# One product of the down projection over both token halves from seven inner products, with sums made by accumulating DMAs

## The chip, the cores and the metric

The kernel runs on one core of one Trainium2 chip. The metric is the device time of one execution in microseconds. The engines are named as the profile names them: PE is TensorE (matmuls), DVE is VectorE, ACT is ScalarE, POOL is GpSimd, and SP only issues DMAs.

## The reference

A token's output mixes a linear attention block `a` and a gated linear unit `b` by a scalar gate `g`. Token count is 2048, width 640, inner width 1536, 32 heads of 20.

```python
x = A_x
g = sigmoid((x * gate_w).sum(-1, keepdims=True))
# a: phi(t) = where(t > 0, t + 1, exp(t)) + 1e-6 of q and k; kv = sum over tokens of phi(k) v
#    o = phi(q) kv / (phi(q) sum phi(k) + 1e-6); a = o @ wo
# b: h = sigmoid(x @ w_gate) * (x @ w_up); b = h @ w_down
return g * a + (1 - g) * b
```

All of it is float32.

## The kernel before

Every float32 product is made from three matmuls: each operand is split in a high part (ACT rounds it, line 215) and a low part (DVE subtracts, line 219), and PE adds high x high, high x low and low x high in PSUM (`mm3`, lines 203 and 205). A matmul has a 128x128 weight and 512 moving columns.

Up to about 510 us the kernel computes the attention's sums, then the gated unit in 12 blocks of 128 rows of `h`, already weighted by `1 - g`; blocks of `phi(q)`, weighted by the attention's factor, are put beside them as further rows, so that one **down projection** gives the sum of both branches. Its weights are `w_down` and the attention's matrix `m`.

The down projection is done in two token halves (`pr` 0 and 1), each of two groups of 512 tokens. Even and odd row blocks and the two token groups make a 2x2 scheme of Strassen's kind, with seven products instead of eight. Their operands on the side of `h` are called B11, B21, T2, T1, T3, B22 and T4: the T forms are sums and differences of h blocks, made on DVE in the gated part and stored to DRAM by POOL (`h_dram`, for each form and half 8 blocks of 128 rows by 512 tokens). On the weight side `sum_s` has stored the sums that belong to them (`s_dram`).

From 510.8 us on only this projection runs. It goes by **h tiles**: an h tile is two of the 8 blocks of one form (128 x 2 x 512 values, 512 KB). Tiles are numbered in the order in which PE takes them; `HQ` is that list, 56 tiles long before the change. For each tile SP loads it into one of three raw buffers (`hw`, `load_h`); ACT and DVE split it into one of five split buffers (`hf`, `queue_h`, `NH = 5`), so that tile k takes the buffer of tile k-5; after the split SP issues the load of tile k+3 into the raw buffer that came free. PE then takes it with the weights of two or three output blocks of 128 columns: 12 or 18 matmuls. Weights come the same way, through two raw buffers `ws` into `wa`. A fifth output block is kept in PSUM tiles `rot`; the others are in `cc`, `dd` and `ch`, two buffers each. When the last tile of a product is done, ACT copies a PSUM tile out (`ot<-ch` and the like) or DVE adds it to an earlier result; POOL stores the finished output (`put`).

T3 is multiplied with the second and fourth output block's weights (`USE["T3"] = ("SE", (1, 3), None)`): for each half 4 tiles of 12 matmuls.

What stands where in an engine's list is decided when the program is written out, by `Order`: it keeps a running estimate of the time of PE, ACT and DVE, and `fill` puts a waiting split into the lists of ACT and DVE when the estimate says that its load has landed (8 us after it was issued, for most tiles) and that it ends no more than a few us behind PE. What PE needs for its next matmul and has not yet been put in is put in at that point (`need`). Engines run their lists in order.

```python
SEQ = [[(1, "B11"), (0, "B11")], [(1, "B21")], [(1, "T4")], [(0, "B21")]]
SEQ += [[(pr, n)] for pr in (1, 0) for n in ("T2", "T1", "T3", "B22")] + [[(0, "T4")]]
HQ = [(pr, n, pp) for turn in SEQ for pp in range(PP) for pr, n in turn]
```

Of the kernel before, what the change touches and what calls it, by code (L numbers as in the profile page):

```python
# [7 lines left out]
F32 = mybir.dt.float32  # L8
# [7 lines left out]
P = 128  # L16
# [162 lines left out]
def gated_mix_kernel(ctx: ExitStack, tc: tile.TileContext, xt, xn, wk, wv, wo, wst_q, wst_f, out_t):  # L179
# [81 lines left out]
    s_dram = [dram.tile([P, 2, TG], F32, name=f"s{p}") for p in range(FC // 2 + 2)]  # L261
    r_dram = [dram.tile([P, 2, TG], F32, name=f"r{pr}") for pr in range(2)]
# [1115 lines left out]

    def raw_down(odd, pp):
# [159 lines left out]
    hooks = {0: begin, 3: den_all}  # L1539
    NH = 5  # L1540
    WA, RAW = {}, {}

    def wd_tile(key, cols):
        pool = PL["ha"] if key == ("E", 0) else PL["wa"]
# [4 lines left out]
    def load_down(key, t=None):  # L1549
# [3 lines left out]
        if kind == "S":  # L1553
            v = t[:, :8 * P].rearrange("p (j o c) -> p j o c", j=2, c=P)
            nc.sync.dma_start(t[:, :8 * P].rearrange("p (j c) -> p j c", j=2), s_dram[n])
# [8 lines left out]
        RAW[key] = v, max(order.pe, order.vec) + (8.0 if kind == "S" else 5.0)  # L1564

    d_loads = [("E", pp) for pp in range(1, PP)] + [("O", pp) for pp in range(4)] + [("L", 0)]
    d_loads += [("S", p) for p in range(2 * PP)]
# [5 lines left out]
    def queue_down(key):  # L1573
# [5 lines left out]
        def s_part(j):  # L1579
            t = wd_tile((("SE", "SO")[j], n // 2), 4)  # L1580
            split(t[:, 0, n % 2], t[:, 1, n % 2], RAW[key][0][:, j])
            if j:
                order.then(next_down)
# [5 lines left out]
        def whole():  # L1589
            if kind == "L":  # L1590
                t = WA[key] = PL["wa"].tile([P, 2, KC + 2, P], F32R, name="wl", tag="wl")
            else:
                t = wd_tile(key, 3 if kind == "E" else KC)
            split(t[:, 0], t[:, 1], RAW[key][0])
            if key != ("E", 0):
                order.then(next_down)

        if kind == "S":
            for j in range(2):
                order.add(a_cost(4 * P), v_cost(4 * P), lambda j=j: s_part(j), ("wa", ("SE", "SO")[j], n // 2), at)  # L1600
        else:
            w = {"E": 6, "O": 10, "L": 7}[kind] * P
# [4 lines left out]
    SEQ = [[(1, "B11"), (0, "B11")], [(1, "B21")], [(1, "T4")], [(0, "B21")]]  # L1607
    SEQ += [[(pr, n)] for pr in (1, 0) for n in ("T2", "T1", "T3", "B22")] + [[(0, "T4")]]
    HQ = [(pr, n, pp) for turn in SEQ for pp in range(PP) for pr, n in turn]
    HF, HR = {}, {}  # L1610

    def load_h(k, tiles=None):
        if k < len(HQ):
            pr, n, pp = HQ[k]
            if tiles:
                for i, t in enumerate(tiles):
                    nc.sync.dma_start(t, h_dram[pr, n][:, 2 * pp + i])
            else:
                tiles = PL["hb"].tile([P, 2, TG], F32, name="hw", tag="hw", bufs=3)
                nc.sync.dma_start(tiles, h_dram[pr, n][:, 2 * pp:2 * pp + 2])  # L1620
            HR[k] = tiles, max(order.pe, order.vec) + (5.0 if k < 5 else 8.0)

# [15 lines left out]
    REST, REST_AT = {}, {13: 0, 20: 1, 36: 0}  # L1638
# [110 lines left out]
    plan += [("S", p) for p in range(2 * PP)]  # L1749
# [4 lines left out]
    hk = done_h = 0  # L1754

    def advance():

        while plan:
# [7 lines left out]
            else:  # L1766
                order.stream = order.mid if kind == "S" else order.items
# [7 lines left out]
    USE = {"B11": ("E", (0, 1), 2), "B21": ("O", (0, 2), 4), "T2": ("SE", (0, 2), None), "T1": ("SO", (1, 3), None),  # L1775
           "T3": ("SE", (1, 3), None), "B22": ("SO", (0, 2), None), "T4": ("O", (1, 3), None)}
# [5 lines left out]
    def mm(ps, wt, wp, col, h, first):  # L1782
# [4 lines left out]
    class Pass:  # L1787
# [23 lines left out]
        def product(self, q, pp, h):  # L1811
            if q is not None:
                mm(self.dst[q], WA[self.kind, pp], (0, 1), self.cols[q], h, self.first and pp == 0)
            elif self.extra is not None:
                mm(self.extra, WA[self.ek, pp], (0, 1), self.ec, h, self.n in ("B11", "B21") and pp == 0)
# [25 lines left out]
        def out(self, q):  # L1841
            pr, n, C = self.pr, self.n, self.C
            if q is not None:
                ps = self.dst[q]
                if n in ("B11", "T2", "T1") or self.own:
                    C[n, q] = out_tile()
                    act(C[n, q], ps, AF.Copy, "q")
                elif n == "T4":
                    self.close(q, ps)
                else:  # L1850
                    o, g = {"B21": (0, self.g0), "T3": (1, self.g1), "B22": (0, self.g1)}[n]
                    t = C.pop(({"B21": "B11", "T3": "T1", "B22": "T2"}[n], q))
# [99 lines left out]
```

## Time and profile before

| | |
|---|---|
| Median of 3 runs | 726.13 us (726.11 to 726.49) |
| Profiled execution | 727.02 us, of which the span is 724.2 |
| First matmul of the down projection | 510.76 us into the span |
| Last matmul | 719.99 us, then the last output block leaves |
| Granted PE clock | 1.00 all through |
| DMA | 144.05 MB, mean 199 GB/s |

The page of the profile gives each engine's busy share of the span. A group's row names the source line, the engine, the operation and what it writes and reads, then the count, the busy time, the mean of one in ns, and what ended the idle time ahead of it. In a timeline row the first two numbers are the start and the duration in us; in brackets stands how long the engine had been idle, and on whom it had waited. A row of the DMA view ends with the median time from issue to landing. In a table of stages each engine's busy time stands with its count of instructions, and the last three columns are the granted clock, the DMA share and GB/s.

### The profile page before, as it was taken

To read this page: it belongs to the slowest core of one execution; us is meant where nothing else is said; L and a number is where in the kernel's file an instruction comes from. 1 tells how busy PE (TensorE), PEld (TensorE's weight loads), DVE (VectorE), ACT (ScalarE), POOL (GpSimd) and SP (SyncE) were. 2 spreads that over 40 slices of the span, in tenths; PEclk is the share of its full clock that TensorE was granted. 3 is DMA by queue.
4 is the path that set the end of the run, shared out by engine and by line. 5 is a ranking of instruction groups with operands and counts; after the bars stand their busy time and mean duration, and the time that the engine had idled before them with its cause. 6 is when DMAs were issued, how large, how long until landed. Compare 5 with 4: busy or idle time off the path is not lost.

```text
span 724.2 us, 9524 instructions
## 1 busy us (share of the span) xinstructions
PE 719.5 (99%) x3411; PEld 607.8 (84%) x3411; DVE 486.3 (67%) x773; ACT 320.5 (44%) x541; POOL 128.9 (18%) x221
## 2 busy tenths in 40 slices
PE   9999999999999999999999999999999999999997
PEld 8999998888888888888888888888888888888886
DVE  4878576868764698678879778786866664434340
ACT  6664637166756233333333232334367644424321
POOL 0311011122520023213224222330200000010000
PEclk9999999999999999999999999999999999999999
DMA  7553536897555474556578658474987975565431
GB/s 253 140 141 70 162 55 159 201 302 247 191 174 182 153 238 126 176 194 242 188 273 299 221 188 294 157 258 143 324 300 259 329 231 190 158 213 194 146 113 72
DMA packets 59491, 144.05 MB, mean 199 GB/s; under 512 B 7310, under 2 KB 20782, under 8 KB 59445
## 3 DMA queue, kind: packets, MB, share of 16 engines
q1 hardware_dynamic: 40757, 88.50, 38.4%
q0 software_dynamic: 18544, 54.83, 23.2%
q8 instruction: 26, 0.43, 0.3%
q14 instruction: 20, 0.16, 0.1%
q10 hardware_dynamic: 144, 0.13, 0.1%
HBM read 89.81 MB, written 49.84 MB: 193 GB/s over the span
## 4 chain that ended last, share of the span: by engine, by line
PE 99%; DVE 0%; ACT 0%; issue 0%
PE ch L205 18%; PE cc L205 17%; PE rot L205 16%; PE dd L205 14%; PE ch L203 9%; PE cc L203 8%; PE rot L203 8%; PE dd L203 7%; PE cc L1136 1%; PE rot L300 0%; PE cc L1216 0%; DVE ot L219 0%; ACT ot L215 0%
## 5 line engine op out<-in xcount | busy, mean ns | idle before, releaser
L219 DVE TENSOR_TENSOR hf<-hw,hf 128x1024 fp32r<-128x1024 f32 x54 | 65.8, 1223 | 68.7 <-ACT hf L215 68.4
L215 ACT ACTIVATE hf<-hw 128x1024 fp32r<-128x1024 f32 x54 | 56.8, 1057 | 53.7 <-PE rot L205 30.5
L219 DVE TENSOR_TENSOR c<-cc,c 128x512 f32<-128x512 f32 x56 | 37.7, 686 | 45.9 <-PE cc L205 40.5
L205 PE MATMUL dd<-hf,wa 128*128 128x512 f32 x160 | 49.3, 389 | 0.0
L205 PE MATMUL ch<-hf,wa 128*128 128x512 f32 x160 | 49.3, 389 | 0.0
L1736 POOL DMA_DIRECT2D out_t<-ot x18 | 9.7, 540 | 183.8 <-DVE ot L219 180.8
L215 ACT ACTIVATE wG<-wst 128x640 fp32r<-128x640 f32 x17 | 12.4, 737 | 65.0 <-PE dd L205 65.0
L215 ACT ACTIVATE c<-ch 128x512 f32<-128x512 f32 x32 | 19.1, 597 | 48.8 <-PE ch L205 44.0
L205 PE MATMUL rot<-hf,wa 128*128 128x512 f32 x128 | 39.4, 389 | 0.0
L205 PE MATMUL cc<-hf,wa 128*128 128x512 f32 x128 | 39.4, 389 | 0.0
L203 PE MATMUL dd<-xrh,wG 128*128 128x512 f32 x90 | 35.3, 393 | 0.0
L205 PEld LDWEIGHTS ch<-hf,wa 128*128 128x128 f32 x160 | 30.0, 188 | 6.3
L205 PEld LDWEIGHTS dd<-hf,wa 128*128 128x128 f32 x160 | 30.0, 188 | 6.3
L205 PE MATMUL dd<-xrh,wG 128*128 128x512 f32 x90 | 35.1, 390 | 0.0
L205 PE MATMUL dd<-xrl,wG 128*128 128x512 f32 x90 | 35.0, 389 | 0.0
L219 DVE TENSOR_TENSOR c<-c,om 128x512 f32<-128x512 f32 x48 | 33.1, 692 | 1.6
L203 PE MATMUL cc<-xbh,wS 128*128 128x512 f32 x84 | 32.7, 389 | 0.0
L205 PE MATMUL cc<-xbl,wS 128*128 128x512 f32 x84 | 32.7, 389 | 0.0
L205 PE MATMUL cc<-xbh,wS 128*128 128x512 f32 x84 | 32.7, 389 | 0.0
L203 PE MATMUL dd<-hf,wa 128*128 128x512 f32 x80 | 31.1, 389 | 0.0
L203 PE MATMUL ch<-hf,wa 128*128 128x512 f32 x80 | 31.1, 389 | 0.0
L215 ACT ACTIVATE c<-rot 128x512 f32<-128x512 f32 x24 | 14.2, 597 | 38.1 <-PE rot L205 30.8
(471 smaller groups left out, 2084.6 us busy)
## 6 DMA issues: line engine op xcount, KB each, us to landing
hf<-p_dram SPq DMA_DIRECT2D x16, 512.0 KB, 4.7
hw<-h1T SPq DMA_DIRECT2D x16, 512.0 KB, 5.4
hw<-h0T SPq DMA_DIRECT2D x16, 512.0 KB, 4.3
wst<-wst_f SPq DMA_DIRECT2D x12, 640.0 KB, 4.7
xst<-xt SPq DMA_DIRECT2D x10, 640.0 KB, 7.0
h1T<-c POOLq DMA_DIRECT2D x24, 256.0 KB, 2.7
h0T<-c POOLq DMA_DIRECT2D x24, 256.0 KB, 3.0
hw<-h1B SPq DMA_DIRECT2D x11, 512.0 KB, 4.5
```

The source lines that it names most:

```text
L203: nc.tensor.matmul(o, l_hi, r, start=first, stop=False, skip_group_check=True)
L205: nc.tensor.matmul(out, a, b, start=False, stop=last and n == 1, skip_group_check=True)
L215: nc.scalar.activation(out, src, fn, **kw)
L219: nc.vector.tensor_tensor(out, a, b, op=op)
L1136: nc.tensor.matmul(ps[:w, b0:b1], v[:, m, :w], g(m), start=(m == 0), stop=(m == KC - 1))
L1736: (eng or nc.gpsimd).dma_start(out_t[o * P:(o + 1) * P, g * TG + c0:g * TG + c1], t[:, c0:c1])
```

## The change

T3's two products, one for each token half, are seen as one product of a 2x2 scheme again: the two output blocks by the two halves of the 8 row blocks, times those two halves of the rows by the two token halves. It is formed in Strassen's way from seven **inner products** P1 to P7 of four row blocks each, that is of two h tiles each, and an inner tile feeds 6 matmuls.

- The operands of P7, P6 and P3 are sums of T3 of both halves. They are made in DRAM (`f_sum`, in two parts) by POOL's DMAs that add to what is there: `f_copy` and `f_add` before P7, another `f_add` between P7 and P6, another between P6 and P3. P5's operand is made in place in `h_dram[0, "T3"]` by `f_low`.
- The weights of the inner products (kind `I`, two sets) are loaded from `s_dram` in four DMAs each; DVE makes four sums of them, and they are split like others. `S` loads now leave out those columns (two DMAs for one). E's weights are split in two parts, `E` and `E2`.
- The results are combined on DVE: P7's, P1's, P6's and P5's are copied out by ACT and added into the PSUM tiles `dd` and `cc` in which P2, P3 and P4 also add up (`Inner.out`, `x_sums`). T3's eviction in `Pass.out` goes; T1's second pass now closes the output blocks that T3 closed.
- The order of tiles is new. After tile 19 (the end of B21 for half 0) come, with + for half 1: P7 P7 T2+ P1 T2+ P1 T2+ T2+ P6 T2 P6 T2 P5 T2 P5 T2 P2 P2 P3 T1+ P3 T1+ P4 T1+ P4 T1+, tiles 20 to 45; then B22+, T1, B22 and T4 as whole products, to tile 61.

```diff
+    f_sum = dram.tile([P, 4, TG], F32, name="f_sum")
...
+    KA, KB = (slice(0, 2), slice(2, 7, 4)), (slice(3, 5), slice(5, 8, 2))
+    KF = (slice(0, 2), slice(2, 4))
...
+    def f_copy(u):
+        nc.gpsimd.dma_start(f_sum[:, KF[u]], h_dram[1, "T3"][:, KA[u]])
+
+    def f_add(u, pr, c):
+        nc.gpsimd.dma_start(f_sum[:, KF[u]], h_dram[pr, "T3"][:, c[u]], accum_op=OP.add)
+
+    def f_low(u):
+        h = h_dram[0, "T3"]
+        nc.gpsimd.dma_start(h[:, KA[u]], h[:, KB[u]], accum_op=OP.add)
...
-    hooks = {0: begin, 3: den_all}
+    hooks = {0: begin, 3: den_all, 5: lambda: f_copy(0), 6: lambda: f_add(0, 0, KA), 11: lambda: f_low(0)}
...
+        elif kind == "I":
+            def at_i():
+                return at() if done_h > 8 else 1e9
+            order.add(a_cost(2 * P), v_cost(2 * P), lambda: i_plain(0), ("wa", "I", n), at_i)
+            order.add(a_cost(4 * P), v_cost(4 * P), lambda: i_plain(1), ("wa", "I", n), at_i)
+            for s in range(4):
+                order.add(0, v_cost(2 * P), lambda s=s: i_sum(s), ("wa", "I", n), at_i)
+            for s in (2, 3):
+                order.add(a_cost(4 * P), v_cost(4 * P), lambda s=s: i_plain(s), ("wa", "I", n), at_i)
...
-    HQ = [(pr, n, pp) for turn in SEQ for pp in range(PP) for pr, n in turn]
+    HQ = [(pr, "B11", pp) for pp in range(PP) for pr in (1, 0)]
+    HQ += whole(1, "B21") + whole(1, "T4") + whole(0, "B21")
+    HQ += mixed("P7 P7 T2+ P1 T2+ P1 T2+ T2+ P6 T2 P6 T2 P5 T2 P5 T2 P2 P2 P3 T1+ P3 T1+ P4 T1+ P4 T1+")
+    HQ += whole(1, "B22") + whole(0, "T1") + whole(0, "B22") + whole(0, "T4")
+    INNER = {"P7": (f_sum, KF), "P6": (f_sum, KF), "P3": (f_sum, KF), "P1": (h_dram[1, "T3"], KA),
+             "P2": (h_dram[1, "T3"], KB), "P5": (h_dram[0, "T3"], KA), "P4": (h_dram[0, "T3"], KB)}
...
+            nxt = {"P7": ("P6", 0, KB), "P6": ("P3", 1, KB)}.get(n)
+            if nxt:
+                key = nxt[0], pp
+                F_DUE[key] = lambda: f_add(pp, *nxt[1:])
+                order.late.append((HR[k][1], lambda: F_DUE.pop(key, int)()))
...
-    REST, REST_AT = {}, {13: 0, 20: 1, 36: 0}
+    REST, REST_AT = {}, {13: 0, 28: 1, 50: 0}
+    F_AT = {6: lambda: f_copy(1), 9: lambda: f_add(1, 0, KA), 20: lambda: f_low(1)}
...
+        def product(self, u, h):
+            w = WI[self.n, u]
+            prod(self.dst, [(w[:, 0, i], w[:, 1, i], h[:, 0, i], h[:, 1, i]) for i in (0, 1)], self.first and u == 0)
+
+        def out(self):
...
+            elif n in ("P2", "P3"):
+                q = int(n == "P3")
+                t = CS[1].pop(("T4", q))
+                add(t, X[1][q], t, "q")
+                put(2 * q + 1, 2, t)
+            if n in IS:
+                act(IS[n], self.dst, AF.Copy, "q")
+            if n == "P6":
+                add(IS["P1"], IS["P6"], IS["P1"], "a")
+                sub(IS["P7"], IS["P1"], IS["P7"])
+                add(X[1][1], X[1][1], IS["P7"])
+            elif n == "P5":
+                add(X[1][1], X[1][1], IS["P5"], "a")
+                add(IS["P5"], IS["P5"], IS["P1"])
...
+    def x_sums(pr):
+        if pr:
+            add(X[1][0], X[1][0], IS["P1"])
+        else:
+            sub(X[0][0], X[0][0], IS["P1"])
+            sub(X[0][1], X[0][1], IS["P5"])
```

How this moves instructions is shown at three places. The numbers in the names are those of buffers in the built program: in the changed kernel the split tiles 20 to 25 are hf_5216, hf_5238, hf_5282, hf_5322, hf_5353 and hf_5372.

ACT, from the eviction of the second column of B21 (half 0) on. Before the change, this was the end of B21 and the start of T2:

```order
L215 ACTIVATE ot_5282<-ch_5166 128x512
L215 ACTIVATE hf_5302<-hw_5232 128x1024
L215 ACTIVATE rot_5307<-ot_4871 128x512
L215 ACTIVATE hf_5321<-hw_5243 128x1024
L215 ACTIVATE hf_5344<-hw_5271 128x1024
```

After the change, at the same place; wa_5379 is the weight of P5's and P7's second tiles, wa_5293 and wa_5359 are those of P1, P2 and P3, and is_5391 takes P7's result:

```order
L215 ACTIVATE ot_5336<-ch_5208 128x512
L215 ACTIVATE hf_5353<-hw_5241 128x1024
L215 ACTIVATE wa_5293<-ws_5271 128x256
L215 ACTIVATE wa_5359<-ws_5271 128x512
L215 ACTIVATE hf_5372<-hw_5285 128x1024
L215 ACTIVATE wa_5379<-ws_5271 128x512
L215 ACTIVATE wa_5381<-ws_5271 128x512
L215 ACTIVATE is_5391<-ch_5365 128x512
```

Four weight splits of the second set of inner weights now stand there, two of them behind the split of tile 25 (hf_5372), which takes the buffer of tile 20.

DVE at the same place. Before, with the closing sums of B21 and the low parts of tiles 23 to 25 (hf_5268, hf_5302 and hf_5321):

```order
L219 TENSOR_TENSOR hf_5268<-hw_5188,hf_5268 128x1024
L219 TENSOR_TENSOR ot_4898<-ot_5282,ot_4898 128x512
L219 TENSOR_TENSOR ot_5295<-rot_5167,ot_4911 128x512
L219 TENSOR_TENSOR hf_5302<-hw_5232,hf_5302 128x1024
L219 TENSOR_TENSOR hf_5321<-hw_5243,hf_5321 128x1024
```

After, from B21's last closing sum (ot_5349, which reads `rot`) on; ws_5271 are the raw inner weights, on which the sums are made in place:

```order
L219 TENSOR_TENSOR ot_5349<-rot_5209,ot_4930 128x512
L219 TENSOR_TENSOR hf_5353<-hw_5241,hf_5353 128x1024
L219 TENSOR_TENSOR wa_5293<-ws_5271,wa_5293 128x256
L219 TENSOR_TENSOR wa_5359<-ws_5271,wa_5359 128x512
L219 TENSOR_TENSOR ws_5271<-ws_5271 128x256 x2
L219 TENSOR_TENSOR hf_5372<-hw_5285,hf_5372 128x1024
L223 SCALAR_TENSOR_TENSOR ws_5271<-ws_5271 128x256
L219 TENSOR_TENSOR ws_5271<-ws_5271 128x256
L219 TENSOR_TENSOR wa_5379<-ws_5271,wa_5379 128x512
```

Three low parts of weights and four sums have come in between, and wa_5379 stands last.

DVE where a product closes. Before, T3 of half 1 (sums from dd_4660 and dd_4661) among the low parts of B22's tiles:

```order
L219 TENSOR_TENSOR ot_5466<-dd_4660,ot_5466 128x512
L219 TENSOR_TENSOR ot_5139<-dd_4660,ot_5139 128x512
L219 TENSOR_TENSOR hf_5546<-hw_5488,hf_5546 128x1024
L219 TENSOR_TENSOR ot_5477<-dd_4661,ot_5477 128x512
L219 TENSOR_TENSOR ot_5155<-dd_4661,ot_5155 128x512
```

After, from P5's end (its result is ot_5585) to P3's; the tiles 35 to 40 are hf_5589 (T2's last), hf_5602 and hf_5623 (P2), hf_5636 (P3), hf_5649 (T1+) and hf_5672 (P3); P2 closes in dd_4667 and P3 in dd_4668:

```order
L219 TENSOR_TENSOR dd_4668<-dd_4668,ot_5585 128x512
L219 TENSOR_TENSOR ot_5585<-ot_5585,is_5391 128x512
L219 TENSOR_TENSOR hf_5589<-hw_5532,hf_5589 128x1024
L219 TENSOR_TENSOR hf_5602<-hw_5555,hf_5602 128x1024
L219 TENSOR_TENSOR cc_4688<-cc_4688,is_5391 128x512
L219 TENSOR_TENSOR cc_4689<-cc_4689,ot_5585 128x512
L219 TENSOR_TENSOR hf_5623<-hw_5577,hf_5623 128x1024
L219 TENSOR_TENSOR ot_5169<-dd_4667,ot_5169 128x512
L219 TENSOR_TENSOR hf_5636<-hw_5592,hf_5636 128x1024
L219 TENSOR_TENSOR hf_5649<-hw_5605,hf_5649 128x1024
L219 TENSOR_TENSOR hf_5672<-hw_5626,hf_5672 128x1024
L219 TENSOR_TENSOR ot_5187<-dd_4668,ot_5187 128x512
```

Sums that read a product which PE has just closed now stand directly ahead of the low part of the tile that PE takes next; behind the last row comes hf_5685, tile 41. On ACT the high part of hf_5589 stands behind P5's eviction, that of hf_5602 behind the eviction of T2's first column, and that of tile 46 (B22's first) behind T1's second.

More of the change, by code (lines that the diff above doesn't have):

```diff
@@ L1563, in load_down @@
                 nc.sync.dma_start(v[:, j], src[:, j])
-        RAW[key] = v, max(order.pe, order.vec) + (8.0 if kind == "S" else 5.0)
+        RAW[key] = v, max(order.pe, order.vec) + (8.0 if kind in "SI" else 5.0)
     d_loads = [("E", pp) for pp in range(1, PP)] + [("O", pp) for pp in range(4)] + [("L", 0)]
-    d_loads += [("S", p) for p in range(2 * PP)]
+    d_loads += [("S", p) for p in range(2 * PP)] + [("I", u) for u in range(2)]
     def next_down():
@@ L1766, in advance @@
             else:
[L1767 removed]
+                order.stream = order.mid if kind in "SI" else order.items
                 queue_down((kind, k))
```

187 lines of the change are left out of this document (140 added, 47 removed).

## The prediction

> **What bounds the kernel now.** I read the page first: the share of the engines and the chain of work that ended last. Then the waits of TensorE, then the timeline around the place where the first changed product will stand, about 592 us.
>
> ```profile
> span 724.2 us, 9524 instructions
> PE 719.5 (99%) x3411; PEld 607.8 (84%) x3411; DVE 486.3 (67%) x773; ACT 320.5 (44%) x541; POOL 128.9 (18%) x221
> ...
> PE 99%; DVE 0%; ACT 0%; issue 0%
> ...
> PE rot L300 <- PEq L1943: 0.8, 1, 0.8
> ```
>
> The last row is the whole answer on what PE waited for: 0.8 us, once, at the start. So before the change the end is set by the matmuls alone, and everything else lies beside them. A removed matmul is worth its full pace; an added wait on PE costs its full length.
>
> ```profile
> 592.36 0.39 PE L203 MATMUL dd<-hf,wa 128*128 128x512 f32 x1
> 592.59 0.62 PE L205 MATMUL dd<-hf,wa 128*128 128x512 f32 x2
> 593.04 0.39 PE L203 MATMUL dd<-hf,wa 128*128 128x512 f32 x1
> ```
>
> The duration of 0.39 us is pipelined; the pace is what counts. Three matmuls start between 592.36 and 593.04, so one costs 0.227 us. 592.36 us is also the start of tile 20, which was T2's first and becomes P7's first.
>
> **What is removed.** T3 was 8 tiles (4 for each token half) of 12 matmuls, 96. Now 14 tiles (7 inner products of two tiles) of 6 matmuls, 84. 12 fewer, 12 x 0.227 = **2.7 us saved**. All else on PE keeps its count.
>
> **What is added beside PE.** Six more tiles to load and split, and the splits are the point:
>
> ```profile
> L219 DVE TENSOR_TENSOR hf<-hw,hf 128x1024 fp32r<-128x1024 f32 x54 | 65.8, 1223 | 68.7 <-ACT hf L215 68.4
> L215 ACT ACTIVATE hf<-hw 128x1024 fp32r<-128x1024 f32 x54 | 56.8, 1057 | 53.7 <-PE rot L205 30.5
> L219 DVE TENSOR_TENSOR c<-cc,c 128x512 f32<-128x512 f32 x56 | 37.7, 686 | 45.9 <-PE cc L205 40.5
> L219 DVE TENSOR_TENSOR ws<-ws 128x256 f32<-128x256 f32 x1 | 0.4, 417 | 0.0
> hw<-h1T SPq DMA_DIRECT2D x16, 512.0 KB, 5.4
> ```
>
> A split is 1.06 us on ACT, then 1.22 us on DVE; a sum of 512 columns is 0.69 us, of 256 columns 0.42 us; a load lands 5.4 us after its issue. An h tile had fed 12 matmuls or more (2.7 us of PE); an inner tile feeds 6 (1.36 us), and with T2's tiles between them the mean is 2.04 us. With three raw buffers a tile can come every (5.4 + 1.06 + 1.22) / 3 = 2.6 us. Five split tiles of lead cover some of that; the lead is used up about where P5 stands. As totals ACT and DVE have room (44% and 67%); what counts is where a split stands in their order, since each engine runs its list in order.
>
> How eviction and PE touch is seen before the change:
>
> ```profile
> 588.48 0.60 ACT L215 ACTIVATE ot<-ch 128x512 f32<-128x512 f32 x1 [3.60 <-PE ch L205]
> ...
> 591.88 1.06 ACT L215 ACTIVATE hf<-hw 128x1024 fp32r<-128x1024 f32 x1 [0.76 <-PE rot L205]
> ...
> 592.56 0.69 DVE L219 TENSOR_TENSOR ot<-rot,ot 128x512 f32<-128x512 f32 x1 [0.68 <-PE rot L205]
> ```
>
> Each starts when PE is done with its bank or tile: the last, 592.56, lies 0.2 us after the next tile's first matmul at 592.36. An eviction is 0.60 us on ACT. In this part of the before kernel the split that runs is for a tile four or five ahead, so an eviction in front of it cost PE nothing. With the new order this cover is gone at seven or eight places; I lay the rows of the new order out in time with the durations above, a row starting when the row ahead of it and what it reads are done (the engine's pace is some 0.1 us shorter than a duration).
>
> *Gap 1, the second tile of P7.* Its weight (wa_5379) is split last of the weights, from sums. On ACT that split stands behind the split of hf_5372, and hf_5372 takes the buffer of P7's first tile, so it cannot start before PE is through with it, at 592.36 + 1.36 + 0.2 = 593.9. DVE is later still. ot_5349 reads the bank that PE ends at 592.56; hf_5353's high half starts at 592.6 on ACT and ends at 593.7; then on DVE its low half to 594.9, two weight rests (256 and 512 columns) to 595.9, two sums of 256 to 596.7, hf_5372 to 597.8, two sums to 598.6, and wa_5379's rest to 599.3. The high half of that weight lets two matmuls go at 597.4, the third waits for 599.3 instead of 594.2: **5.1 us**. The weights' own load comes in time: it follows the last split of the S weights, which ended at 586.1 before the change (rows below), and such a load lands in 5.8 us, so by 592; its first split on ACT stands behind hf_5353, at 593.6.
>
> ```profile
> 584.77 1.29 DVE L219 TENSOR_TENSOR wa<-ws,wa 128x512 fp32r<-128x512 f32 x2
> ...
> ws<-s SPq DMA_DIRECT2D x5, 512.0 KB, 5.8
> ```
>
> *Gap 2, P5's first tile.* Its split stands behind P6's eviction and three sums that hang on each other: 0.2 + 0.6 + 3 x 0.69 + 1.22 = 4.1 us after P6; T2's tile between covers 2.7 + 0.2. **1.2 us**.
>
> *Gap 3, T2's last tile.* It follows P5 at once; its split (hf_5589) stands behind P5's eviction and two sums: 0.2 + 0.6 + 2 x 0.69 + 1.22 = 3.4, due at 0.2. **3.2 us**.
>
> *Gaps 4 and 5, P2's tiles.* hf_5602 stands on ACT behind T2's first eviction: 0.2 + 0.5 + 1.06 + 1.22 = 3.0 after that column, due after the second column at 1.6: **1.4 us**. hf_5623 stands on DVE behind the two sums into cc, 1.2 us after hf_5602; P2's six matmuls cover part: **0.9 us**.
>
> *Gaps 6 and 7, P3's first tile and T1's second.* On DVE the closing sum of P2 (ot_5169), and later that of P3 (ot_5187), waits for the product to end, and the next tile's low half stands behind it: 0.2 + 0.6 + 1.22 = 2.0, due at 0.2. **1.8 us each**; the tile after P3's first loses some 0.4 more.
>
> *Gap 8, B22's first tile* stands behind T1's second eviction, like gap 4: **1.4 us**. After it a tile feeds 18 matmuls (4.1 us) against a supply of 2.6, and the lead comes back; I cost the rest at nothing.
>
> Sum of the gaps: 5.1 + 1.2 + 3.2 + 1.4 + 0.9 + 1.8 + 1.8 + 0.4 + 1.4 = 17.2 us. The gaps add up because each stands after a product that PE has just ended, so an earlier gap doesn't shorten a later one.
>
> **What no row of before shows.** DMAs that accumulate from DRAM into DRAM (six, with two copies and two in place as well). Nearest rows:
>
> ```profile
> d<-hf POOLq DMA_DIRECT2D x8, 128.0 KB, 4.3
> s<-hf POOLq DMA_DIRECT2D x8, 512.0 KB, 3.5
> ```
>
> The first holds six that accumulate. Bounds for a 512 KB one: 3.5 us, as a plain store, and 4 x 4.3 = 17 us, if it scales with the bytes. The tightest use has over 20 us (P6's sum can start when P7's loads land, near 575 us, and its load is issued near 598), so I take nothing; they only take bandwidth. A gain is excluded, since nothing that PE waits for was a DMA.
>
> ```profile
> 510.00:530.00 20.00, 20.00 (x90) 16.56 (x89) 14.26 (x18) 8.66 (x10) 4.79 (x9) 1.00 0.98 333
> ...
> 590.00:610.00 20.00, 20.00 (x90) 16.57 (x89) 10.89 (x11) 9.49 (x13) 1.62 (x3) 1.00 0.65 207
> ```
>
> The last two columns are the DMA share and GB/s. From 590 on there is room for the six tiles more (3 MB) and the sums. Near 520, where the copy and the first sum of f_sum's second part fall, the engines are full; a tile there may come a few us late. PE keeps 4.1 us on each tile then and the lead is several tiles: nothing, or at most 3 us. On POOL the sums stand in the queue between stores; the in-place sum of f = 11 waits for a store just issued, about 3 us, and the stores behind it have no reader for tens of us: nothing. Splitting E's weights and the S loads in two adds short rows at tens of us from their use: nothing.
>
> The clock is the other unknown. PE's first matmuls, before any steady work:
>
> ```profile
> 0.85 3.32 PE L300 MATMUL rot<-const-bfloat16-1.0 128*128 128x512 bf16 x9 [0.85 <-PEq L1943]
> ...
> 4.08:6.00 1.92, 1.92 (x11) 1.49 (x11) 1.40 (x3) 0.89 (x2) 0.00 (x0) 1.00 0.91 271
> 6.00:8.00 2.00, 2.00 (x15) 2.00 (x15) 0.69 (x3) 1.19 (x4) 0.00 (x0) 1.00 1.06 305
> ```
>
> Eight and a half of 512 columns took 3.23 us to the next start, 0.38 each, against 0.227 later, though the granted clock reads 1.00 throughout. So after rest PE ran slow for some 4 us, losing 3.23 - 8.5 x 0.227 = 1.3 us and a little after. Gap 1 leaves PE at rest from about 594 to 597.4. Bounds: nothing, or 2 us; I take nothing, since no row shows that a rest inside the run does it. [...]
>
> **The sum.** The profiled execution took 727.02 us (span 724.2 and 2.8 around it), 0.9 above the median of 726.13. 727.0 - 2.7 + 17.2 = 741.5 by that execution, 740.6 by the median. I forecast **741 us**, 2% slower.
>
> **Rivals.**
>
> *No gaps.* One mechanism: the splits keep their lead of four or five tiles through the inner products, as in T2 and T3 before, where all PE waits were zero. Place: ACT and DVE from 592 us. Then only the 12 matmuls count: 726.1 - 2.7 = 723.4 us. It decides where all gaps together stay under 2.7 us. For it: both engines' idle time. Against: the order puts a row that waits for PE's last product directly ahead of the split that PE needs next, and no speed of the loads changes that. 11%: 7% with gaps under 1.2 us in all, 4% with 1.2 to 4.2 us, which is 0.2% (1.5 us) to either side of no change.
>
> *Only the weights' gap.* While PE stands 5 us, loads and splits run ahead, and gaps 2 to 8 shrink to little: 726.1 - 2.7 + 5.1 to 8 = 728.5 to 731.5. For it: rows on ACT and DVE without PE in them do get ahead. Against: gaps 3, 6 and 7 don't depend on a lead. 13%.
>
> *Half clock after gap 1, or loads late as well.* PE starts again after gap 1 as it started at 0.85 us, which costs 1.3 to 2 us, and with loads that land late too (some six tiles at 0.5 us or more, DMA being at 0.65 of its time here) 742 to 748. For it: a rest of over 3 us. Against: loads have 2 us to spare at most tiles. 15%. [...]
>
> *The change's sums come late.* It would do what it says on PE, but P6, P3 or P5 wait for an accumulated sum; at over 22 us each, where 17 is the bound above, that is 5 us or more on top, 746 and up. 4%.
>
> Forecast with its own range, 735 to 745: 57%. The range of 8 in 10 takes in most of the weights' gap alone and of the half clock: **729 to 747**. About 0.2% is what a measurement of this kernel can tell from no change. By the cases: faster 7%, within it 4%, slower 89%.
>
> **What would show it.** PE's count falls by 12 (3399). PE's waits, one row before, show in `ch` a wait for DVE or ACT of about 5 us near 594, and some eight more of 1 to 3 us up to 670; their sum is near 17. If their sum is under 3 us, my reading of the order is wrong; if gap 1 is there and gaps 3, 6 and 7 are not, the second rival holds. A pace of 0.4 us after the first gap would show the clock; a wait of PE, ACT or SP for f_sum would show the late sums.

## The result, and the profile after

The changed kernel takes 747.61 us (median of 5 runs, 747.03 to 748.40) against 726.13: 1.0294 times the time of before, 95% interval 1.0279 to 1.0309. The forecast was 741 us, range 729 to 747.

The page of the kernel after: span, busy time of the engines, and the chain that ended last.

```profile
span 745.9 us, 9627 instructions
PE 724.6 (97%) x3399; PEld 608.3 (82%) x3399; DVE 504.3 (68%) x807; ACT 330.3 (44%) x563; POOL 139.0 (19%) x231
...
PE 93%; DVE 3%; DMA 1%; issue 1%; ACT 1%; SPq 0%; DVEq 0%; ACTq 0%
```

PE has its 12 matmuls fewer, yet is busy 5.1 us longer than before. The chain is no longer PE's alone. The waits of PE in the kernel after (total, times, longest):

```profile
PE ch L203 <- ACT wa L215: 5.3, 1, 5.3
PE ch L205 <- DVE hf L219: 3.6, 3, 1.7
PE dd L205 <- DVE hf L219: 3.1, 3, 1.7
PE cc L203 <- ACT hf L215: 1.7, 1, 1.7
PE cc L205 <- DVE hf L219: 1.2, 1, 1.2
...
PE ch L203 <- ACT ot L215: 0.8, 1, 0.8
PE ch L205 <- DVE wa L219: 0.6, 1, 0.6
PE ch L203 <- ACT hf L215: 0.3, 1, 0.3
```

Twelve rests, 16.6 us, where the forecast summed 17.2. That leaves 5.1 + 2.7 = 7.8 us in which PE counts as busy and does nothing more. The timeline of PE in the kernel after shows where, behind gap 1 and behind gap 3:

```profile
600.56 0.79 PE L203 MATMUL ch<-hf,wa 128*128 128x512 f32 x1 [5.29 <-ACT wa L215]
...
602.43 0.80 PE L205 MATMUL ch<-hf,wa 128*128 128x512 f32 x1 [0.65 <-DVE wa L219]
603.03 0.63 PE L203 MATMUL ch<-hf,wa 128*128 128x512 f32 x1
...
606.01 0.70 PE L205 MATMUL dd<-hf,wa 128*128 128x512 f32 x2
606.55 0.39 PE L203 MATMUL dd<-hf,wa 128*128 128x512 f32 x1
...
635.70 0.50 PE L203 MATMUL cc<-hf,wa 128*128 128x512 f32 x1 [1.69 <-ACT hf L215]
637.35 1.22 PE L205 MATMUL cc<-hf,wa 128*128 128x512 f32 x2 [1.15 <-DVE hf L219]
...
640.64 0.40 PE L203 MATMUL cc<-hf,wa 128*128 128x512 f32 x1
```

From 602.43 to 606.55 PE starts 10 matmuls, 0.41 us each; at 0.227 they would take 2.27 us, so 1.85 are lost, and some 0.75 more on the two from 600.56 to the rest of 0.65 us (1.87 - 0.65 - 0.45). From 637.35 to 640.64 it starts 8, which loses 1.5. That is **4.1 us of half pace**: PE starts a matmul every 0.43 us instead of every 0.227. The granted clock, third column from the end, is 0.50 in just these two stretches of the kernel after:

```profile
599.33:606.16 6.83, 4.95 (x11) 3.46 (x12) 3.71 (x8) 2.88 (x5) 0.00 (x0) 0.50 1.05 261
636.88:640.29 3.41, 2.94 (x7) 2.36 (x8) 0.42 (x1) 0.40 (x1) 0.00 (x0) 0.50 0.44 151
```

PE is busy for 4.95 + 2.94 us in them, which at 0.43 instead of 0.227 us a matmul loses 3.7 us. The other 0.4 of the 4.1 belong to the toll that follows.

The rest is a toll on each stop. At gap 2 the row ahead of it starts at 626.96 and the next two are these:

```profile
628.46 0.74 PE L205 MATMUL ch<-hf,wa 128*128 128x512 f32 x2 [1.11 <-DVE hf L219]
629.04 0.40 PE L203 MATMUL ch<-hf,wa 128*128 128x512 f32 x1
```

Three matmuls should take 0.68 us from start to start; they took 2.08. The stop costs 1.40, of which 1.11 are written as idle: **0.29 us more**, since the last matmul runs out (0.39 against a pace of 0.227) and the first two behind the stop take 0.58 us from start to start (628.46 to 629.04) instead of 0.45. Twelve of these make 3.5 us. The sum: -2.7 + 16.6 + 4.1 + 3.5 = 21.5 us; the spans differ by 745.9 - 724.2 = 21.7. Some 0.4 us are counted twice in it, and the toll of one stop is taken for all twelve, so it closes to about half a us and no better.

### The profile page after: what moved, and what is told of

Same layout as the page of the kernel before. It is cut to its first block, busy times and chain, and to the rows that moved or that the text cites. A ratio compares the mean times of both kernels' runs of the same rounds, so it can differ in the third digit from the quotient of the medians.

```text
span 745.9 us, 9627 instructions
## 1 busy us (share of the span) xinstructions
PE 724.6 (97%) x3399; PEld 608.3 (82%) x3399; DVE 504.3 (68%) x807; ACT 330.3 (44%) x563; POOL 139.0 (19%) x231
## 4 chain that ended last, share of the span: by engine, by line
PE 93%; DVE 3%; DMA 1%; issue 1%; ACT 1%; SPq 0%; DVEq 0%; ACTq 0%
PE ch L205 18%; PE cc L205 16%; PE rot L205 15%; PE dd L205 13%; PE ch L203 9%; PE cc L203 8%; PE rot L203 8%; PE dd L203 6%; DVE hf L219 1%; DMA ws<-s 1%; PE cc L1137 1%; ACT hf L215 1%; PE rot L301 1%; DVE wa L219 0%; DVE ws L219 0%
## 5 line engine op out<-in xcount | busy, mean ns | idle before, releaser
L219 DVE TENSOR_TENSOR hf<-hw,hf 128x1024 fp32r<-128x1024 f32 x60 | 72.6, 1223 | 48.8 <-ACT hf L215 48.4
L215 ACT ACTIVATE hf<-hw 128x1024 fp32r<-128x1024 f32 x60 | 62.5, 1055 | 40.3 <-PE rot L205 10.5
L205 PE MATMUL ch<-hf,wa 128*128 128x512 f32 x192 | 60.8, 398 | 4.2 <-DVE hf L219 3.6
L205 PE MATMUL dd<-hf,wa 128*128 128x512 f32 x144 | 45.2, 396 | 3.1 <-DVE hf L219 3.1
L205 PEld LDWEIGHTS ch<-hf,wa 128*128 128x128 f32 x192 | 36.4, 191 | 13.4 <-DVE hf L219 4.7
L203 PE MATMUL ch<-hf,wa 128*128 128x512 f32 x96 | 38.3, 399 | 6.4 <-ACT wa L215 5.3
L219 DVE TENSOR_TENSOR wa<-ws,wa 128x512 fp32r<-128x512 f32 (+2 forms) x34 | 22.3, 681 | 19.4 <-ACT wa L215 19.0
L205 PEld LDWEIGHTS dd<-hf,wa 128*128 128x128 f32 x144 | 27.3, 191 | 9.9 <-DVE hf L219 4.3
L205 PE MATMUL cc<-hf,wa 128*128 128x512 f32 x104 | 33.2, 401 | 1.2 <-DVE hf L219 1.2
L215 ACT ACTIVATE wa<-ws 128x512 fp32r<-128x512 f32 (+2 forms) x34 | 19.9, 621 | 31.5 <-DMA ws<-mp_dram 10.7
```

Source lines behind the costliest of these rows:

```text
L203: nc.tensor.matmul(o, l_hi, r, start=first, stop=False, skip_group_check=True)
L205: nc.tensor.matmul(out, a, b, start=False, stop=last and n == 1, skip_group_check=True)
L215: nc.scalar.activation(out, src, fn, **kw)
L219: nc.vector.tensor_tensor(out, a, b, op=op)
```

## The experiments

The kernel before was run again beside each group of experiments and took 726.47 to 726.89 us there; the changed kernel was not run again, so a difference under 1 us to its 747.61 tells nothing.

**The clock.** Is the slow pace brought by the rest, or by something else near gap 1? First, rests without the change, in the kernel before:

```diff
+    STOP = {21: 5, 26: 1, 31: 3, 36: 8, 41: 2, 46: 4, 50: 6}
...
+            if q == 1 and k in STOP:
+                for _ in range(STOP[k]):
+                    lo = HF[k][:, 1, 0]
+                    nc.vector.tensor_tensor(lo, f32(lo), f32(lo), op=OP.max)
             b.product(q, pp, HF[k])
```

> The kernel before the change, with seven rests of PE put in between the first and second column of seven tiles of the down projection, far apart: 5, 1, 3, 8, 2, 4 and 6 DVE rows of 0.6 us each (an identity on the low part that PE needs next), so rests of some 0.9 to 5.1 us. Nothing else of the change is in it. Theory A (after a long rest PE starts at half pace): the short rests cost themselves and 0.3 us of refill, the rests of some 2.5 us and more are followed by about 5 us of matmuls at 0.43 us each instead of 0.227, 2 us more for each; 29 x 0.6 + 7 x 0.8 + 4 x 2 = 31 us, so 757 us. Theory B (the slow matmuls after gap 1 come from something else there, its weights or its transfers): pace 0.227 right after each rest, 726 + 23 = 749 us.

761.86 us, one run. Six of the rests show (the single row at tile 26 never stopped PE), 24.8 us in all, longer than planned. Two of them in the timeline of PE:

```profile
690.96 0.73 PE L205 MATMUL dd<-hf,wa 128*128 128x512 f32 x2 [2.21 <-DVE hf L1901]
691.52 0.40 PE L203 MATMUL dd<-hf,wa 128*128 128x512 f32 x1
691.76 0.62 PE L205 MATMUL dd<-hf,wa 128*128 128x512 f32 x2
...
712.12 0.74 PE L205 MATMUL cc<-hf,wa 128*128 128x512 f32 x2 [1.83 <-DVE hf L1901]
...
712.94 0.63 PE L205 MATMUL cc<-hf,wa 128*128 128x512 f32 x2
713.41 0.56 PE L203 MATMUL cc<-hf,wa 128*128 128x512 f32 x1
713.77 1.06 PE L205 MATMUL cc<-hf,wa 128*128 128x512 f32 x2
...
717.05 0.40 PE L203 MATMUL cc<-hf,wa 128*128 128x512 f32 x1
```

Theory A holds, but not by the length of the rest: behind 2.21 us the pace is 0.23 at once; behind 1.83 us PE runs at full pace for 1.3 us and only then falls to 0.43, until 717.0. The four rests of 4.3 to 7 us are followed by half pace at once, one of them 0.4 us later. A run with many rests was to tell what decides:

```diff
-    STOP = {21: 5, 26: 1, 31: 3, 36: 8, 41: 2, 46: 4, 50: 6}
+    STOP = {k: 3 for k in range(20, 55, 2)}
```

> The kernel before the change with a rest of PE in every second tile of the down projection from tile 20 to 54 (18 rests, each of three DVE rows of 0.6 us, so 1.5 to 2.5 us long). In the run with seven rests a rest of 1.83 us was followed by half pace and one of 2.21 us was not; the half pace ended at 604.2, 645.5, 675.8, 716.8 and 737.3 us, all of them a whole number of steps of 3.41 us apart. Theory A (PE's activity is judged in fixed windows of 3.41 us: half pace begins at the end of a window that was idle for more than about half of it, and ends at the end of the first wholly busy one): rests that lie within one window for more than 1.7 us bring half pace, those that a window's end cuts do not; both kinds occur among the 18, without a clean limit in length, and all ends of half pace lie on one grid of 3.41 us. Theory B (the length of the rest alone decides): one length parts the two kinds. The time itself: 18 rests of 2 us, 18 x 0.3 us of refill, and half pace behind 4 to 12 of them at 1 to 2.5 us each: 771 to 795 us.

797.38 us, one run, 2 above what was expected; sixteen rests show, of 1.1 to 5.1 us, and twelve episodes of half pace. Two rests in the timeline of PE:

```profile
596.55 0.73 PE L205 MATMUL dd<-hf,wa 128*128 128x512 f32 x2 [2.38 <-DVE hf L1901]
597.12 0.40 PE L203 MATMUL dd<-hf,wa 128*128 128x512 f32 x1
...
642.37 0.74 PE L205 MATMUL dd<-hf,wa 128*128 128x512 f32 x2 [2.88 <-DVE hf L1901]
...
646.83 0.63 PE L205 MATMUL dd<-hf,wa 128*128 128x512 f32 x2
```

The twelve ends (the first rows at full pace, 609.45, 622.90, 646.83 and so on to 773.24) are 13.45, 23.93, 10.27, 10.24, 13.66, 17.19, 10.29, 10.28, 23.78, 17.03 and 13.67 us apart: 4, 7, 3, 3, 4, 5, 3, 3, 7, 5 and 4 steps of 3.41 us, none off by more than 0.2 us. The granted clock goes by the same grid: below it is 0.50 from 643.29 to 646.70 and so rises 0.13 us ahead of the row at 646.83. In the kernel after, its two stretches at 0.50 (599.33 to 606.16 and 636.88 to 640.29) are two steps and one long and start eleven apart. Here are the stretches around the two rests; behind the comma stands PE's busy time, and the granted clock is third from the end:

```profile
592.09:595.50 3.41, 2.08 (x10) 1.38 (x8) 2.84 (x4) 1.40 (x2) 1.08 (x2) 1.00 0.77 160
595.50:598.92 3.42, 2.37 (x10) 1.97 (x11) 0.96 (x2) 0.91 (x1) 0.00 (x0) 1.00 1.04 413
...
639.88:643.29 3.41, 0.92 (x4) 0.78 (x5) 2.36 (x4) 0.00 (x0) 0.00 (x0) 1.00 0.44 132
643.29:646.70 3.41, 3.41 (x10) 2.63 (x9) 1.23 (x1) 1.06 (x1) 0.00 (x0) 0.50 0.05 22
```

The rest that ends at 596.55 is cut into 1.3 and 1.1 us and brings nothing, though it is longer than the 1.83 us of the run before, which lay within one step; that of 2.88 us is cut into 0.4 and 2.5 us and brings half pace from the next line of the grid on, 643.29. In these runs the clock thus changed on a grid of 3.41 us: 1.83 us of rest in one step were followed by half pace, 1.69 us (gap 7 of the kernel after) were not, and half pace ended behind a step with little rest or none (0.47 us in the one from 636.88 in the kernel after, none in that from 643.29). What lies between, the runs don't tell apart: 0.83 and 0.92 us in one step brought half pace in the run with all three edits below, while some 1.75 us in one step brought none in the run without the sums (an estimate from where half pace ends in that run, some 638.5 us, and the steps of 3.41 us).

Then the changed kernel, with its two long rests filled by matmuls whose result is overwritten:

```diff
+                if (n, pp) == ("P7", 1):
+                    idle(24, IB["u"], HF[k][:, 0, 0])
...
+            if k == 35 and q == 0:
+                idle(15, IB["t"], REST[1][:, 0, 0])
```

> The changed kernel with matmuls whose result is overwritten in two of its rests: 24 in gap 1 (between P7's two tiles, into the bank that P1 opens later) and 15 ahead of T2's last tile (gap 3). All else stands where it stood. Theory A (half pace after rest): PE goes on at 0.227 us per matmul behind both, which saves about 2.4 us behind gap 1 and 1.5 us behind gap 3, less what the inserted rows overrun: 743.5 to 745 us against 747.6. Theory B (the pace there is set by something else): the matmuls behind still start 0.43 us apart, 747.6 us or a little more.

745.68 us, 1.9 less though PE does 39 matmuls more. Behind gap 1 the timeline of PE reads:

```profile
603.00 0.50 PE L205 MATMUL ch<-hf,wa 128*128 128x512 f32 x1 [1.14 <-DVE wa L219]
603.34 0.39 PE L203 MATMUL ch<-hf,wa 128*128 128x512 f32 x1
603.57 0.63 PE L205 MATMUL ch<-hf,wa 128*128 128x512 f32 x2
```

The same matmuls, behind the same wait, now start 0.23 us apart, at a granted clock of 1.00. Theory B falls. The gain stays under the 4.1 us of half pace. From the row behind this wait to the one behind gap 2 PE takes 24.3 us (603.00 to 627.32) instead of 26.0 (602.43 to 628.46), 1.7 less. At gap 3 the inserted rows end late and a new rest of 0.27 us follows, so only 0.8 are saved. And 0.6 us had been lost ahead of P7, which starts at 594.20 here and at 593.62 in the changed kernel.

**Gap 1.** Two edits give the weights time: two tiles of T2 ahead of P7, or the two inner sets ahead of the last two S loads.

```diff
-    HQ += mixed("P7 P7 T2+ P1 T2+ P1 T2+ T2+ P6 ...
+    HQ += mixed("T2+ T2+ P7 T2+ P7 P1 P1 T2+ P6 ...
```

> The changed kernel with the inner tiles moved back by some tiles of T2: T2+ T2+ P7 T2+ P7 P1 P1 T2+ P6 and so on as before, so that the second set of inner weights is due at about 602 us and not at 595. Theory A (gap 1 is the weights' lateness and brings its slow restart): gap 1 (0.8 + 5.3 + 0.65 us) shrinks to 0 to 2 us and the half pace behind it goes too (2.4 us), 739 to 742 us. Theory B (the splits are late there whatever the order of tiles is): the rest moves to P7's second tile or to P1, 746 to 749 us.

```diff
-    plan += [("S", p) for p in range(2 * PP)] + [("I", u) for u in range(2)]
+    plan += [("S", p) for p in range(6)] + [("I", u) for u in range(2)] + [("S", p) for p in (6, 7)]
```

(and `d_loads` in the same way)

> The changed kernel with the loads and splits of the two sets of inner weights taken ahead of the last two loads of S (six S loads, the two sets, the last two S loads, which T2's last tile needs at about 606 us). The order of tiles is that of the change. Theory A (gap 1 is the late second set, the half pace behind it comes from that rest, and the rest of the gaps does not depend on it): the wait for the bank, gap 1 and its remainder (0.8 + 5.3 + 0.65 us) go, and with them 2.4 us of half pace; 738 to 740.5 us, gaps 2 to 8 as before. Theory B (the time that gap 1 gave to loads and splits is missed behind it, as in the run with two tiles of T2 first): new rests of the same sum between 600 and 635 us, 745 to 748 us.

747.42 and 744.95 us, 0.2 and 2.7 less. Gap 1 is gone in both, wholly: nothing waits for `wa` any more. But new rests stand behind it, in the timeline of PE with two tiles first:

```profile
622.20 0.49 PE L203 MATMUL cc<-hf,wa 128*128 128x512 f32 x1 [1.63 <-ACT hf L215]
624.57 1.22 PE L205 MATMUL cc<-hf,wa 128*128 128x512 f32 x2 [1.87 <-DVE hf L219]
```

They bring half pace too (1.22 us for two), and so does a pair of 1.63 and 0.76 us ahead of them, near 612 us. With the sets first the new rests stand near 620 us, 1.63 and 1.86 us, with half pace behind them again; all rests sum to 12.2 us instead of 16.6. So gap 1 was the weights' lateness, but theory B is nearer on the price: in gap 1 loads and splits had got ahead, and what it gave them was missed at tile 31.

**Gaps 2 to 8.** Two ways to write the splits ahead of the rows that wait for PE:

```diff
-            HR[k] = tiles, max(order.pe, order.vec) + (5.0 if k < 5 else 8.0)
+            HR[k] = tiles, max(order.pe, order.vec) + (5.0 if k < 5 or k >= 24 else 8.0)
```

> The changed kernel with the planner's estimate of a load's landing at 5 us instead of 8 from tile 24 on, so that the splits are written ahead of the evictions and sums that wait for PE, where the list allows it (P5's first tile and T2's last tile above all). Theory A (gaps 2 to 8 are made by the place of splits in the lists): gaps 2 and 3 go (1.1 + 2.8 us, and 1.5 us of half pace behind gap 3), some of gaps 4 to 8 too; 738 to 742.5 us. Theory B (the loads through three raw buffers set these gaps): the splits wait for their loads at the same times, 746 to 748 us.

```diff
                 if pp == 1:
-                    b.out()
+                    later.append((k + 1, b.out))
```

(T2's evictions and `x_sums` likewise; `later` runs when the next tile's product is written)

> The changed kernel with the evictions and sums that close an inner product or T2 written one tile later, behind the split that PE needs next. Theory A (gaps 2 to 7 are the place of these rows): the rests of 1.1, 1.7 + 1.15, 0.76, 0.68, 1.68 and 1.69 us go or shrink to under 0.5, and 1.5 us of half pace behind gap 3 with them; 739 to 742 us. Theory B (the loads through three raw buffers decide): the splits wait for their loads instead, 746 to 748 us.

743.33 and 742.31 us, 4.3 and 5.3 less. With the sums later, these are the waits of PE:

```profile
PE ch L203 <- ACT wa L215: 4.0, 1, 4.0
PE ch L203 <- ACT ot L215: 3.1, 1, 3.1
PE cc L205 <- DVE hf L219: 1.4, 1, 1.4
...
PE ch L205 <- DVE hf L219: 0.8, 1, 0.8
...
PE dd L205 <- DVE hf L219: 0.2, 1, 0.2
```

Of the nine rests behind gap 1, three are left (1.40, 0.24 and 0.76 us); two new ones near 700 us are taken up below. Their cause was the place of the rows, as forecast. The gain is less than those rests since gap 1 itself grew, to 3.1 + 4.0 + 0.65 us, and the granted clock is 0.50 from 595.7 to 609.3. A longer gap 1 also lets loads and splits run ahead, but that is not what removed the rests: the run with all three edits, below, has no gap 1 and only 2.0 us of rests between 625 and 660 us, where the changed kernel has 8.8.

**The accumulating DMAs.** Costed at nothing in the prediction. Left out:

```diff
-        nc.gpsimd.dma_start(f_sum[:, KF[u]], h_dram[pr, "T3"][:, c[u]], accum_op=OP.add)
+        pass
```

(the same in `f_low`)

> The changed kernel without any accumulating DMA (f_add and f_low do nothing; the two plain copies into f_sum stay), so T3's operands lack their sums. Theory A (the two sums for P6, issued at 577.3 and 579.9 us, and their like take the DMA engines from the first set of inner weights, which then lands after 9.3 us and not after some 5.5): that set lands near 585 us, its splits end before P7 begins, gap 1 shrinks by 3 us or more and the wait for the bank of P7 goes; 741 to 744 us. Theory B (gap 1 hangs on the order of the second set's rows behind PE's own progress, and the accumulation takes only bandwidth that nobody misses): 747 to 748 us, gap 1 still 5 us and more.

745.11 us, 2.5 less, and gap 1 is 3.0 + 1.0 us, without the 0.8 ahead of it. In the kernel after, POOL issues two sums while the first inner set is on its way; the timeline of POOL, then the chain of work (start, length, what), then the DMA view of that set's loads alone (count, KB, median us to landing), first with the sums, then without:

```profile
577.32 0.88 POOL L1390 DMA_DIRECT2D f_sum<-h0T  x1 [11.82 <-DMA hw<-f_sum]
579.93 1.19 POOL L1390 DMA_DIRECT2D f_sum<-h0T  x1 [1.73 <-DMA hw<-f_sum]
```

```profile
580.05 9.28 DMA ws<-s
589.35 0.64 ACT wa L215
```

```profile
ws<-s SPq DMA_DIRECT2D x4, 128.0 KB, 9.3
```

```profile
ws<-s SPq DMA_DIRECT2D x4, 128.0 KB, 3.7
```

Without the sums ACT splits that set from 583.57 us on, in the kernel after from 589.02. A rival was the small pieces of that load. The weights' sums were stored so that it reads runs of 1 KB instead of 512 B (`even_cols` is laid out to match):

```diff
-        nc.gpsimd.dma_start(s_dram[p], st["st"])
+        for k in range(2):
+            nc.gpsimd.dma_start(even_cols(p, k), (e0, e1)[k])
+        nc.gpsimd.dma_start(s_dram[p][:, 1], st["st"][:, 1])
```

> The changed kernel with the sums of the weights stored so that the columns of S and those of the inner products each stand in runs of 1 KB rather than 512 B (the same bytes; the eight stores become three DMAs each). Theory A (the 9.3 us that the first set of inner weights took to land are the price of its 512 B pieces on busy DMA engines): it lands some 3 us sooner, the wait for P7's bank goes and gap 1 is 2.5 to 3.5 us as in the run without the sums; 744 to 746 us. Theory B (the accumulating DMAs beside it set that landing): 9 us and 747 us as before.

749.38 us, and the load in the chain lands after 9.65 us instead of 9.28. The pieces are not it.

**All together.** The sets first, the estimate and the later sums in one kernel:

> The changed kernel with the inner weights' sets ahead of the last S loads, the estimate of a load's landing at 5 us from tile 24 on, and the closing rows one tile later. Theory A (the three causes add up and the 12 matmuls are a gain once the rests are gone): 724 to 728 us. Theory B (with all these gone the loads through three raw buffers cannot follow tiles of 2.04 us on the mean, as the lead of five tiles is used up near tile 32): rests of 5 to 10 us in all between 625 and 665 us, 731 to 737 us.

737.34 us, 10.3 less. Alone the three gained 2.7, 4.3 and 5.3 us, some 12 in all, and two of them move the same splits; theory B describes what is left. Two rows of its PE waits, also there in the two runs with earlier splits, had come with the edits:

```profile
PE dd L205 <- DVE hr L219: 0.9, 1, 0.9
...
PE dd L203 <- ACT hr L215: 0.8, 1, 0.8
```

```diff
-        ... lambda at=order.pe + (8.0 if done_h < 13 else 11.0): at, lazy=True)
+        ... lambda at=order.pe + (8.0 if done_h < 13 else 5.0 if done_h > 40 else 11.0): at, lazy=True)
```

> The kernel of the run with all three edits, and the last split of the remaining rows (hr, for half 0) due 5 us and not 11 us after its load's issue. Theory A (the waits of 0.83 and 0.92 us near 695 us with the half pace behind them are that estimate): they go, 733.5 to 735 us. Theory B (the split stands behind other rows there): 737 us.

732.88 us; both rows are gone. With the stores in runs of 1 KB on top:

> The same with the stores in runs of 1 KB. Theory A (loads held up by small pieces make the rest of 2.75 us at tile 31 near 618 us): that rest shrinks by 1 to 3 us with its half pace, 729 to 732 us. Theory B (the accumulating DMAs for P3's operand, issued at 608 and 612 us just as that tile's load is, hold it up): the rest stays, 733.5 to 735 us.

734.16 us: no help here either. What was still open is what makes the six rests that remain (5.5 us, 615 to 638 us):

> The kernel of the run with the three edits and the earlier hr, without any accumulating DMA (T3's operands lack their sums). Its seven rests (1.43, 0.77, 0.76, 1.43, 0.48, 0.66 us and one of PE's start) stand between 615 and 638 us, where its loads landed 5 to 9.5 us after issue. Theory A (the accumulating DMAs hold up those loads): the rests go but for one or two, 724 to 727.5 us. Theory B (three raw buffers and tiles of 2.04 us on the mean make them, whatever else the DMA engines do): 731 to 733 us.

728.06 us, 4.8 less. In the stage from 610 to 625 us the DMA engines' share, the last column but one, falls; first with the sums, then without:

```profile
610.00:625.00 15.00, 11.98 (x48) 8.55 (x47) 6.79 (x7) 7.30 (x11) 1.16 (x1) 1.00 0.98 281
```

```profile
610.00:625.00 15.00, 13.41 (x58) 10.43 (x56) 9.25 (x10) 8.89 (x12) 0.00 (x0) 1.00 0.75 232
```

Four rests are left, 0.74, 1.44, 0.26 and 0.68 us. The account closes: 726.5 - 2.7 + 3.1 + 4 x 0.29 = 728.1. For the same kernel with its sums it gives 726.9 - 2.7 + 5.5 + 6 x 0.29 = 731.4, against 732.05 in the profiled execution and 732.88 in the median; what the rest is, no profile shows. Then the order with a large tile between the inner ones (sums back in), and one sum earlier:

```diff
-    ... P5 T2 P5 T2 P2 P2 P3 T1+ P3 T1+ P4 T1+ P4 T1+")
+    ... P5 T2 P5 T2 P2 T1+ P2 T1+ P3 T1+ P3 T1+ P4 B22+ P4 B22+ B22+ B22+")
...
-    F_AT = {6: lambda: f_copy(1), 9: lambda: f_add(1, 0, KA), 20: lambda: f_low(1)}
+    F_AT = {6: lambda: f_copy(1), 9: lambda: f_add(1, 0, KA), 11: lambda: f_low(1)}
```

> The same kernel with its sums, and from P2 on each inner tile followed by a tile of T1 or B22, which feeds 18 matmuls: P2 T1+ P2 T1+ P3 T1+ P3 T1+ P4 B22+ P4 B22+. Theory A (the rests are short supply: two tiles per 5.4 us is what loads and splits keep up with): those behind P2's first tile (1.43, 0.48, 0.66 us, with 0.3 us of refill each) go, the two near 616 to 623 us stay; 729 to 730.5 us. Theory B (each closing row that waits for PE makes its rest wherever it stands): 732 to 733 us.

> As the run before it, with the second in-place sum (f_low) issued after tile 10 rather than after tile 19, so that it doesn't run beside the loads of tiles 25 to 28. Theory A (that sum, 10.1 us long from 597 us, holds up the loads behind the rests of 1.43, 0.77 and 0.76 us): these shrink, 727 to 729 us. Theory B (the DMA engines are full from 510 to 625 us, and what is moved ahead delays the weights' loads as much): 729.5 to 732 us.

732.13 and 733.37 us. Of the three rests behind 625 us one is left (0.99 us), but the one at 617.8 us grew to 2.42 and brought half pace. The sum moved ahead gained nothing: the rest of 2.42 shrinks to 1.81 us and brings no half pace, but PE now waits 2.19 us at 549.4, where loads run beside the moved sum, and half pace follows there, which is what its theory B says. Last, the spread order without the sums:

> The spread order without any accumulating DMA (T3's operands lack their sums): the change with all its rests' causes taken away. Theory A (nothing else is in the change but 12 matmuls fewer): 723.4 to 725.5 us, that is faster than before by 0.2 to 0.5%. Theory B (the new splits and sums cost something by themselves): 727 us and more.

726.07 us, ratio 1.000 (0.9988 to 1.0013). One short rest (0.51 us) is left in the down projection; by the account it should be 726.5 - 2.7 + 0.8 = 724.6. Runs went from 725.31 to 730.09; the profile is of the slowest, and shows a wait of 3.4 us in the gated part that no other profile has, with half pace behind it (granted clock 0.50 from 152.2 to 155.6). Without both, an estimate, it would have taken some 725.2. Where the missing 1.5 us of the median are, I can't say; the time lies between the two theories. No version with its sums in place came below the kernel before.

## Why the prediction was right and wrong

The order of the rows and the gaps that it makes were read rightly. The forecast fell short by two terms: half pace after rests, which was set at nothing and came to 4.1 us, and the toll of each stop, which was no term and came to 3.5.

- **Saved matmuls**: 12, as forecast. Their 2.7 us are in the accounts above that close; no run shows them by themselves.
- **Gaps**: 16.6 us against 17.2, and at the places named. Gap 2 came out at 1.11 us (1.2 forecast), gap 3 at 2.84 (3.2), gaps 4 and 5 at 0.76 and 0.68 (1.4, 0.9), gaps 6 and 7 at 1.68 and 1.69 (1.8 each), gap 8 at 1.04 (1.4). Moving the rows removed most of gaps 2 to 8, which shows the cause. That the sums agree so well is luck: gap 1 was 1.6 us longer than forecast, and the others together 2.3 shorter.
- **Gap 1** came out at 0.80 + 5.29 + 0.65 us against 5.1. The second set's load, of which I wrote that it "comes in time", did so: ACT never waited for it. What failed is that my working put nothing ahead of it for the first set. That set's loads took 9.3 us (3.7 without the sums that POOL issued beside them), so its splits and sums came when DVE was due at gap 1's rows: DVE began ot_5349 at 596.3 instead of 592.6. The order I had laid out held: without the sums PE had the second set's weight at 598.9, against 599.3 in the working, and 4.0 us of gap 1 remain.
- **The clock**: "Bounds: nothing, or 2 us; I take nothing" is the mis-sized term. It was 4.1 us (3.7 by the granted clock alone): 2.6 behind gap 1, above the upper bound, and 1.5 behind gap 3, where I had not looked, since I had not joined two rests of 1.69 and 1.15 us into one. The granted clock of 1.00 that I read beside the slow start was no evidence: the clock's record in that trace begins only at 3.56 us.
- **Each stop's own toll**, 0.29 us, was no term at all: 3.5 us. I counted idle time as the cost of a wait, where start to start is what counts.
- **Accumulating DMAs**, "so I take nothing": the bounds of 3.5 to 17 us held (6.6 to 10.8 us each), and no reader came too early. But they load the DMA engines: 2.5 us in the changed kernel, 4.8 where other causes are gone.
- **Gaps that add up**: true of the cause, not of the repair. With gap 1 removed, loads and splits had less lead, and part of it came back at tile 31. The rival "only the weights' gap" fell, as gaps 6 and 7 stood. The rival of half clock and late loads, 742 to 748 us, has the right time in part by luck: its half clock came, larger than it said, but of its late loads the runs show only the first set's, and the toll of the stops makes up the rest.

## What to carry to other kernels

Cost a wait of PE from matmul start to matmul start, not by its idle time, and look for half pace behind it: here 1.83 us of rest within one of the steps of 3.41 us in which the granted clock changed were followed by it and 1.69 us were not, and short rests near each other counted together (0.83 and 0.92 us in the run with all three edits). Before an algorithm trades matmuls for smaller operands, count what an operand has to feed: here, at 6 matmuls a tile, splits and closing sums that had been hidden behind 12 made PE wait. DMAs off the path were not free where the DMA engines' share was 0.98 (610 to 625 us with its sums, above) or 1.06 (580.05 to 589.33 us in the kernel after); price them by the loads that run beside them.

## What the runs showed of the hardware beyond that

An accumulating DMA of 512 KB from DRAM to DRAM took 8.8 us (`f_sum<-h0T`, median of four) and 9.6 in place (median of two); the two for P3 took 6.6 and 7.1. A plain store of that size from SBUF took 3.3 (`s<-hf`), but a plain copy within DRAM took 6.7 (`f_sum<-h1T` in the run without sums, median of two). So, as an estimate from these, the adding is worth at most some 2 us, and the larger part of the difference to a store lies in copying within DRAM; the traffic beside them was not the same.

Halving the number of pieces of a load did not bring it in sooner (9.65 us against 9.28, where the DMA engines' share was 1.06 in the kernel after, 580.05 to 589.33 us).
